# Half of tile 0's first product from words, the first low words of W on POOL, one form kept through the ring's tiles, and gate's first sums after T1's load

## The chip, the core and the metric

The kernel runs on one core of one Trainium2 chip. The engines of a core run side by side and wait for each other by semaphores: PE multiplies matrices, DVE and ACT compute elementwise and read PSUM, POOL (GpSimd) computes elementwise on SBUF alone and issues some transfers, and SP issues the other transfers (DMA). The metric is the device time of one execution in microseconds (us), as the median of several runs.

## The reference

One block: layer norm, linear attention with 32 heads, a gated feed-forward part, and a residual.

```python
xn = _layernorm(x, axis=-1)                    # x: 2048 x 576
# linear attention, H = 32 heads of 18
q, k, v = xn @ wqkv, split by heads
pq, pk = phi(q), phi(k)                        # phi(t) = (t + 1 if t > 0 else exp(t)) + 1e-6
kv = einsum("bhsd,bhse->bhde", pk, v); z = pk summed over s
o = (pq @ kv) / (pq . z + 1e-6)
s = o @ wo
# feed-forward, Df = 4608
g = xn @ w_gate; u = xn @ w_up
g = silu((gelu(g) * u) @ w_down)
return x + s * g
```

## The kernel before

Precision comes from words. A float32 operand is cut into a high word (rounded by ACT to the type fp32r) and a low word (what remains, subtracted by DVE or POOL), and a product is a sum of seven passes of word products. `x_mm_plain` instead multiplies float32 as it is, which takes PE two instructions for each product.

The 2048 rows are 16 tiles of 128, in four blocks of 512. The 576 columns are two halves of 288, so x has parts called B11, B21, B12 and B22 (half j of block b), each held as words (`xo`) and plain (`xf`). W for k and v comes as six pieces (c, j), column group c and half j. The text calls them the first (0, 0), second (0, 1), third (1, 0), fourth (1, 1), fifth (2, 0) and last (2, 1). Their loads are interleaved with those of x.

The order on each engine is the order of the code (`pin` and `keep_in_program_order`), so a step that waits holds all that stands behind it on its engine.

The program has these stages:

1. The head, lines 1266 to 1340: tiles 0 to 2 are normalized (`spread` for the statistics, `scales` for the factor, `center`), turned on PE (`turn`) and cut into words (`place`); `save` copies the plain x. `kv_hi` and `kv_lo` cut W's pieces. `x_mm` makes a tile's k and v products, `k_post` and `v_post` finish them (pk, va), `kv_mm` sums them up. Tile 0 is multiplied plainly for piece c = 0, so it can start before any words are there.
2. Tiles 2 to 7 in `kv_tile`. From tile 4 on a tile is turned only in its mean and factor (ms), and normalized on DVE (`normalize`, within `place`).
3. The q phase for blocks 0 and 1: eight `q_store`, each a product on PE and a phi on ACT, DVE and POOL (e_q, ph). The table `behind` says what is recorded after each. There lie the forms: a form is a sum of x's parts (T1, T2, T3, T4 for the fast matrix product later), cut into words by `build` in the big buffer 12 and kept in device memory by `keep`. There too lie the preparations of tiles 8 to 11.
4. Tiles 8 to 15 and the q phase for blocks 2 and 3.
5. The s phase: attention's output `s_mm` for four blocks of four tiles. The table `aside` says what is recorded after each. `den` computes a block's denominators and writes their words (`aux`); `scale` and `halve` use them; `back` loads a kept form; `mat_sums(0)` forms, on POOL, the sums of gate's first matrix.
6. The gate and up matrices, then the down products.

Short-lived tiles come from rings: `slot` gives one of four tiles under the tag h (pk, va, and later pq), `bank` one of six PSUM banks.

Of the kernel before, what the change touches and what calls it, by code (L numbers as in the profile page):

```python
# [8 lines left out]
F32 = mybir.dt.float32  # L9
# [7 lines left out]
P = 128  # L17
# [8 lines left out]
TBN = S // TB  # L26
# [64 lines left out]
def block_kernel(ctx, tc, x, xe, xt, wq_d, wkv_d, wo, wgu_d, wd_d, out):  # L91
# [6 lines left out]
    def bank(name):  # L98
        return ps.tile([P, 512], F32, tag="one", bufs=6, name=name)
# [10 lines left out]
    def slot(shape, dt, name):  # L110
        return sb.tile(shape, dt, tag="h", bufs=4, name=name)
# [15 lines left out]
    def mm(*args, **kw):  # L127
        pin(nc.tensor.matmul(*args, **kw))  # L128
# [24 lines left out]
    def load_x(n, k):  # L153

        if n % 2 == 0:
            shape = [P, 2, 2, 3 * P] if n < TT else [P, 2, D + 6 * P]
            xstat[n // 2] = big(14 + n // 2 % 2, shape, F32, f"x_{n}")
        t = xstat[n // 2][:, n % 2 : n % 2 + k]
        if n < TT:
            dma(out=t, in_=xe[n * P : (n + k) * P].rearrange("(t p) j d -> p t j d", p=P))  # L160
        else:
            dma(out=t[:, :, 0:D], in_=x[n * P : (n + k) * P].rearrange("(t p) d -> p t d", p=P))
            dma(out=t[:, :, D:], in_=xt[n : n + k].rearrange("t p m -> p t m"))
# [32 lines left out]
    def center(n):  # L196

        if n >= TT:
            return
        xs = xstat[n // 2][:, n % 2]  # L200
        m, r = scale_of.pop(n)
        vec("tensor_scalar", xs, xs, m, r, op0=ALU.subtract, op1=ALU.mult)

    def turn(n, new=bank):

        xs = xstat[n // 2][:, n % 2]
        if n >= TT:
            xts[n] = t = bank(f"ms_{n}")
            for i, v in enumerate(scale_of.pop(n)):
                pin(nc.tensor.transpose(  # L210
                    t[:, i * P : (i + 1) * P], v.to_broadcast([P, P]), ident
                ))
            return
        tiles = [new(f"xt_{n}_{j}") for j in range(2)]
        xts[n] = [t[:, 0 : 3 * P].rearrange("p (k t) -> p k t", k=3) for t in tiles]
        for j in range(2):
            for k in range(3):
                pin(nc.tensor.transpose(xts[n][j][:, k, :], xs[:, j, k * P : (k + 1) * P], ident))
# [22 lines left out]
    def place(n, js=(0, 1), words=(0, 1)):  # L241

        tb, t = divmod(n, TT)
        s, b = divmod(tb, 2)
        c = slice(t * P, (t + 1) * P)
        if n >= TT:
            normalize(n, s, b, c)
            return
        for j in js:
            nm = BS[b][j]  # L250
            if nm not in xo[s]:
                xo[s][nm] = big(2 * b + j, [P, 5, TBN], F32R, f"xo_{s}_{nm}")
            o, v = xo[s][nm], xts[n][j]
            if 0 in words:
                act(o[:, 0:3, c], v, AF.Copy)
            if 1 in words:
                vec("tensor_sub", o[:, 3:5, c], v[:, 0:2, :], o[:, 0:2, c].bitcast(F32))
                r = slice(KR, 2 * KR)
                vec("tensor_sub", o[r, 2, c], v[r, 2, :], o[r, 2, c].bitcast(F32))

    def save(n, js=(0, 1), last=True):

        tb, t = divmod(n, TT)
        s, b = divmod(tb, 2)
# [57 lines left out]
    def load_kv(c, j):  # L322
        n = KV.index((c, j))
        if n % 2 == 0:
            raws["kv", n // 2] = big((2, 3, 12)[n // 2], [P, 2, 3, TM], F32, f"rw_{n}")
        raws[c, j] = raws["kv", n // 2][:, n % 2, :, 0 : TW[c]]
        dma(out=raws[c, j], in_=wkv_d[c, j][:, :, 0 : TW[c]])

    def kv_hi(c, j):
        n = KV.index((c, j))  # L330
        if n < 5:
            act(wkv[n][:, 0:3, 0 : TW[c]], raws[c, j], AF.Copy)
        else:
            for i in range(3):
                act(kv_part(c, j, i), raws[c, j][:, i, :], AF.Copy)

    def kv_lo(c, j, eng, mixed=(False, True)):

        n, raw, r = KV.index((c, j)), raws[c, j], slice(2 * KR, 3 * KR)
        if False in mixed:  # L340
            if n < 5:
                hi, lo = (wkv[n][:, i : i + 2, 0 : TW[c]] for i in (0, 3))
                eng("tensor_sub", lo, raw[:, 0:2, :], hi.bitcast(F32))
            else:
                for i in range(2):
                    eng(
                        "tensor_sub", kv_part(c, j, 3 + i), raw[:, i, :],
                        kv_part(c, j, i).bitcast(F32),
                    )
        if True in mixed:  # L350
            o = kv_part(c, j, 2)[r]
            eng("tensor_sub", o, raw[r, 2, :], o.bitcast(F32))
# [48 lines left out]
    KV_PASSES = [(0, 0), (1, 1), (3, 0), (4, 1), (0, 3), (1, 4), (2, 2)]  # L401
    pkv, pks, vas, es, qt = {}, {}, {}, {}, {}

    def x_mm(t, c):

        tb, i = divmod(t, TT)
        s, b = divmod(tb, 2)
        pkv[t, c] = o = bank(f"kv_{t}_{c}")
        for j in range(2):
            for n, (wi, xi) in enumerate(KV_PASSES):  # L410
                mm(
                    o[:, 0 : TW[c]], xo[s][BS[b][j]][:, xi, i * P : (i + 1) * P], kv_part(c, j, wi),
                    start=(j == 0 and n == 0), stop=(j == 1 and n == len(KV_PASSES) - 1),
                )

    def x_mm_plain(js, ks):

        if (0, 0) not in pkv:
            pkv[0, 0] = bank("kv_0_0")
        for j in js:  # L420
            for k in ks:
                r = slice(0, P if k < 2 else KR)
                mm(
                    pkv[0, 0][:, 0 : TW[0]], xf[0][BS[0][j]][r, k, 0:P], raws[0, j][r, k, :],
                    start=(j == 0 and k == 0), stop=(j == 1 and k == 2),
                )

    def k_post(t, c, by_act=False):

        if c == 0:  # L430
            pks[t] = slot([P, D], F32, f"pk_{t}")
            es[t] = tmp([P, D], f"e_k{t}")
        o, e, src = pks[t], es[t], pkv[t, c]
        cs = slice(0, TW[0]) if c == 0 else slice(TW[0], D)
        src = src[:, 0 : cs.stop - cs.start]
        if by_act:
            act(e[:, cs], src, AF.Relu, scale=-1.0)
        else:
            vec("tensor_scalar", e[:, cs], src, 0.0, None, op0=ALU.min)
        vec("tensor_scalar", o[:, cs], src, 0.0, EPS, op0=ALU.max, op1=ALU.add)  # L440
        if c == 1:
            es.pop(t)
            act(e, e, AF.Exp, scale=-1.0 if by_act else 1.0)
            pool("tensor_add", o, o, e)
# [835 lines left out]
    load_kv(2, 0)  # L1280
    load_x(3, 1)
    load_kv(2, 1)

    spread(0, 1)
    kv_hi(0, 0)
    scales(0)
    center(0)
    turn(0, own_bank)
    save(0, (0,), False)
    spread(1, 1)  # L1290
    save(0, (1,), False)
    kv_lo(0, 0, vec)
    x_mm_plain((0,), range(3))
    scales(1)
    center(1)
    x_mm_plain((1,), (0,))
    turn(1)
    x_mm_plain((1,), (1, 2))
    kv_hi(0, 1)
    kv_lo(0, 1, vec)  # L1300
    place(1)
    kv_hi(1, 0)
    kv_lo(1, 0, pool)
    x_mm(1, 0)
    place(0)
    xts.pop(0)
    load_x(4, 2)
    kv_hi(1, 1)
    kv_lo(1, 1, vec)
    save(1)  # L1310
    x_mm(1, 1)
    k_post(0, 0, True)
    k_post(1, 0, True)
    kv_hi(2, 0)
    kv_lo(2, 0, pool)
    kv_hi(2, 1)
    spread(2, 1)
    kv_lo(2, 1, vec)
    scales(2)
# [13 lines left out]
    v_post(0, 2)  # L1333
    center(3)
    v_post(1, 2)
    make_masks()

    def x_next(n):

# [45 lines left out]
    def form(nm):  # L1385
        keep(0, nm, build(0, nm, 12))

    behind = {
        (0, 0): [lambda: kv_mm(N0 - 1), lambda: spread(N0, 2), lambda: difference(0, 3)],
        (0, 1): [  # L1390
            lambda: scales(N0), lambda: form("T1"), lambda: q_store(1, 4),
        ],
        (0, 3): [lambda: turn(N0)],
        (1, 0): [lambda: form("T3"), lambda: place(N0)],
        (1, 1): [lambda: spread(N0 + 2, 2), lambda: scales(N0 + 2)],
        (1, 2): [lambda: form("T2")],
    }
    for tb in range(2):
        for gi in range(NHG - 1):
# [38 lines left out]
    def first_matrix():  # L1438
# [12 lines left out]
        (3, 1): [lambda: scale(0, 0, 1), lambda: halve(0, 0, 1), lambda: back("B11")],  # L1451
        (3, 2): [lambda: scale(0, 2, 3, 4), lambda: halve(0, 2, 3, 4)],
        (3, 3): [lambda: build(1, "T4", X_SLOT["T4"]), lambda: back("T2")],
        (0, 0): [lambda: den(1), lambda: mat_sums(0)],
        (0, 1): [lambda: scale(1, 0, 1), lambda: halve(1, 0, 1)],
        (0, 2): [lambda: scale(1, 2, 3, 4), lambda: halve(1, 2, 3, 4)],
        (0, 3): [lambda: back("T1")],
        (1, 0): [lambda: pieces.extend(first_matrix()), lambda: run(pieces[0])],
        (1, 1): [lambda: run(pieces[3])],
    }  # L1460
# [79 lines left out]
```

## Time and profile before

| | us |
|---|---|
| median of 3 runs | 1469.98 |
| lowest and highest | 1468.36, 1470.25 |
| profiled execution, its own time | 1467.89 |
| its span in the trace | 1466.2 |
| POOL busy | 578.2 |
| first DMA landing read by DVE | 3.98 |

A row of the timeline has the start in us, the length in us, the engine, the line (often a helper's: 122 is ACT's, 125 DVE's, 128 PE's, 131 POOL's, 134 the DMA's), the operation, output<-input by the program's names, shapes, and how many such instructions follow each other. Brackets say how long the engine stood idle before, and what ended it; "issue" means that the profile shows nothing it waited for. A wait is listed as engine, line, what it waited for, us in total, times and longest. A row of the stages has the stretch, its length, the busy time and count of each engine, the granted clock of PE, the DMA engines' busy share and GB/s. PEld is PE's weight load.

### The profile page before, as it was taken

How to read it: one execution, taken by the hardware profiler on the slowest of the kernel's cores; microseconds unless marked ns; L12 is line 12 of the kernel's file. 1: busy time of each engine (PE TensorE's matmuls, PEld its weight loads, DVE VectorE, ACT ScalarE, POOL GpSimd, SP SyncE). 2: the span in 40 equal slices, each digit the busy share in tenths (PEclk: the TensorE clock that was granted, in tenths of full speed). 3: DMA queues.
4: the chain of work that ended last, by engine and by line, in shares of the span. 5: the costliest groups of instructions: out<-in, count | busy, mean ns of one | idle time of the engine just before them, and what ended most of it. 6: DMA issues, size and time to landing. Idle time of an engine off the chain costs nothing.

```text
span 1466.2 us, 21844 instructions
## 1 busy us (share of the span) xinstructions
PE 1454.2 (99%) x8130; PEld 1296.8 (88%) x8130; DVE 1152.6 (79%) x1602; ACT 561.1 (38%) x911; POOL 578.2 (39%) x513
## 2 busy tenths in 40 slices
PE   9999999999999999999999999999999999999998
PEld 7988989988888888888888888888889999999998
DVE  7678577466878788878778887778788988989897
ACT  5344255432232332322333223322335556545454
POOL 3342340125755666656675665757632000000000
PEclk9999999999999999999999999999999999999999
DMA  5445005442243324334152242323379888867886
GB/s 200 181 177 207 11 2 186 166 166 87 94 151 108 111 84 138 110 114 135 51 180 94 94 141 78 148 87 107 137 257 350 267 258 252 252 186 234 278 289 217
DMA packets 117636, 233.96 MB, mean 160 GB/s; under 512 B 10954, under 2 KB 44362, under 8 KB 115482
## 3 DMA queue, kind: packets, MB, share of 16 engines
q1 hardware_dynamic: 114874, 220.51, 45.0%
q0 software_dynamic: 2656, 12.06, 2.2%
q8 instruction: 64, 1.05, 0.3%
q14 instruction: 42, 0.34, 0.1%
HBM read 149.91 MB, written 82.58 MB: 159 GB/s over the span
## 4 chain that ended last, share of the span: by engine, by line
PE 95%; DVE 3%; ACT 1%; issue 1%; POOL 0%; ACTq 0%; DVEq 0%; POOLq 0%
PE bd L128 24%; PE al L807 16%; PE ga L807 16%; PE de L807 16%; PE be L807 8%; PE kv L128 7%; PE s L128 4%; PE q L128 3%; PE kv_a L128 1%; DVE sx L125 1%; PE d L128 0%; PE kw L128 0%; PE idle L1272 0%; PE b L128 0%; ACT xo_T L122 0%
## 5 line engine op out<-in xcount | busy, mean ns | idle before, releaser
L131 POOL TENSOR_TENSOR sm<-raw 128x384 f32<-128x384 f32 x72 | 75.5, 1048 | 148.6 <-DMA raw<-in_wgu_dram 112.2
L128 PE MATMUL kv<-wkv,xo_B 128*128 128x388 f32 (+2 forms) x658 | 127.5, 349 | 2.7 <-ACT xo_B L122 2.6
L125 DVE TENSOR_TENSOR wa<-sm,wa 128x768 fp32r<-128x768 f32 x72 | 95.1, 1321 | 36.1 <-ACT wa L122 35.3
L128 PEld LDWEIGHTS kv<-wkv,xo_B 128*128 128x128 f32 x658 | 118.8, 188 | 4.6 <-ACT xo_B L122 3.0
L128 PE MATMUL bd<-w_head,hi 128*128 128x288 f32 x516 | 117.9, 294 | 0.0
L125 DVE TENSOR_TENSOR wa<-raw,wa 128x256 fp32r<-128x256 f32 x72 | 68.1, 945 | 50.7 <-ACT wa L122 49.6
L125 DVE TENSOR_TENSOR wb<-raw,wb 128x256 fp32r<-128x256 f32 (+1 forms) x108 | 101.0, 935 | 7.4 <-ACT wb L122 5.8
L122 ACT ACTIVATE hi<-raw_h 128x1024 fp32r<-128x1024 f32 x59 | 62.4, 1059 | 92.8 <-PE bd L128 66.3
L128 PE MATMUL bd<-w_end,hi 128*128 128x288 f32 x448 | 89.8, 294 | 0.0
L122 ACT ACTIVATE spot_h<-spot_h 128x512 f32<-128x512 f32 x49 | 30.8, 633 | 149.4 <-DVE spot_h L125 149.4
L125 DVE TENSOR_TENSOR raw_h<-raw_h,hi 128x1024 fp32r<-128x1024 f32 x59 | 71.8, 1220 | 19.5 <-ACT hi L122 19.4
L128 PEld LDWEIGHTS bd<-w_head,hi 128*128 128x128 f32 x516 | 87.0, 188 | 0.1
L128 PE MATMUL bd<-w_end,raw_h 128*128 128x288 f32 x264 | 77.9, 295 | 0.0
L122 ACT ACTIVATE wa<-sm 128x1152 fp32r<-128x1152 f32 x36 | 41.8, 1161 | 91.0 <-PE de L807 91.0
L122 ACT ACTIVATE u<-al 128x512 f32<-128x512 f32 x72 | 41.0, 592 | 90.0 <-PE al L807 65.1
L128 PEld LDWEIGHTS bd<-w_end,hi 128*128 128x128 f32 x448 | 71.9, 188 | 0.0
L128 PE MATMUL bd<-beside,raw_h 128*128 128x288 f32 x240 | 70.8, 295 | 0.0
L131 POOL TENSOR_TENSOR spot_h<-spot_h,spot_h 128x512 f32<-128x512 f32 x45 | 62.6, 1397 | 2.9 <-DVE spot_h L125 2.4
L807 PE MATMUL al<-xo_B,wa 128*128 128x512 f32 x252 | 63.0, 389 | 0.0
L807 PE MATMUL de<-xo_T,wa 128*128 128x512 f32 x252 | 63.0, 389 | 0.0
L807 PE MATMUL ga<-xo_B,wb 128*128 128x512 f32 x252 | 63.0, 389 | 0.0
L807 PE MATMUL de<-xo_T,wb 128*128 128x512 f32 x252 | 63.0, 389 | 0.0
(270 smaller groups left out, 4058.5 us busy)
## 6 DMA issues: line engine op xcount, KB each, us to landing
raw_h<-hs SPq DMA_DIRECT2D x176, 256.0 KB
raw<-in_wgu_dram SPq DMA_DIRECT2D x36, 768.0 KB
hs<-spot_h SPq DMA_DIRECT2D x90, 256.0 KB
hs<-spot_g SPq DMA_DIRECT2D x80, 256.0 KB
b<-in_wd_dram SPq DMA_DIRECT2D x42, 432.0 KB
hs<-spot_m SPq DMA_DIRECT2D x38, 256.0 KB
raw_g<-hs SPq DMA_DIRECT2D x22, 256.0 KB
kept_T<-xo_T SPq DMA_DIRECT2D x4, 1280.0 KB
```

Source lines behind the costliest of these rows:

```text
L122: pin(nc.scalar.activation(*args, **kw))
L125: pin(getattr(nc.vector, op)(*args, **kw))
L128: pin(nc.tensor.matmul(*args, **kw))
L131: pin(getattr(nc.gpsimd, op)(*args, **kw))
L807: nc.tensor.matmul(o, w[0:rows, wi, :], xop[0:rows, xi, :], start=(start and n == 0), stop=(n == len(PASSES) - 1), skip_group_check=True,)
```

## The change

In the head, half 0 of tile 0 is still multiplied plainly, as the first three products; half 1 comes from words, after tile 1 has been turned, by `x_mm` with `js=(1,)` and the passes in an order that asks for W's low words late. The first low words of W, (0, 0), are cut by POOL in place of DVE, and the masks are made at POOL's start. Half 1 of tile 0 is placed before tile 1, half 0 after W's fourth piece, and the copies `save` come after W's last piece.

```diff
+    make_masks()
     spread(0, 1)
     kv_hi(0, 0)
     scales(0)
     center(0)
+    kv_lo(0, 0, pool)
     turn(0, own_bank)
     save(0, (0,), False)
     spread(1, 1)
-    save(0, (1,), False)
-    kv_lo(0, 0, vec)
-    x_mm_plain((0,), range(3))
+    place(0, (1,), (0,))
     scales(1)
     center(1)
-    x_mm_plain((1,), (0,))
+    place(0, (1,), (1,))
+    x_mm_plain()
+    kv_hi(0, 1)
     turn(1)
-    x_mm_plain((1,), (1, 2))
-    kv_hi(0, 1)
     kv_lo(0, 1, vec)
-    place(1)
     kv_hi(1, 0)
     kv_lo(1, 0, pool)
+    place(1)
+    x_mm(0, 0, (1,), sorted(KV_PASSES, key=lambda i: (i[0] > 1) + (i[0] == 2)))
     x_mm(1, 0)
-    place(0)
-    xts.pop(0)
-    load_x(4, 2)
     kv_hi(1, 1)
     kv_lo(1, 1, vec)
-    save(1)
+    place(0, (0,))
+    load_x(4, 2)
     x_mm(1, 1)
+    kv_hi(2, 0)
+    kv_lo(2, 0, pool)
     k_post(0, 0, True)
     k_post(1, 0, True)
-    kv_hi(2, 0)
-    kv_lo(2, 0, pool)
     kv_hi(2, 1)
+    save(0, (1,))
+    save(1)
...
-    make_masks()
```

In the q phase T3 moves up by three q products and is made in three tiles of the ring h in place of buffer 12, with three transfers out. T2 moves up to the place before the statistics of tile 10.

```diff
+    def form_apart(nm):
+
+        f = xf[0][nm]
+        store[0, nm] = d = dr.tile([P, 5, TBN], F32, name=f"kept_0_{nm}")
+        hi, lo, last = (slot([P, 2, TBN], F32R, f"xo_0_{nm}_{i}") for i in range(3))
+        act(hi, f[:, 0:2], AF.Copy)
+        act(last[:, 0], f[:, 2], AF.Copy)
+        vec("tensor_sub", lo, f[:, 0:2], hi.bitcast(F32))
+        r = slice(KR, 2 * KR)
+        vec("tensor_sub", last[r, 0], f[r, 2], last[r, 0].bitcast(F32))
+        dma(out=d[:, 0:2], in_=hi.bitcast(F32))
+        dma(out=d[:, 3:5], in_=lo.bitcast(F32))
+        dma(out=d[:, 2], in_=last[:, 0].bitcast(F32))
...
     behind = {
         (0, 0): [lambda: kv_mm(N0 - 1), lambda: spread(N0, 2), lambda: difference(0, 3)],
...
+        (0, 2): [lambda: form_apart("T3")],
         (0, 3): [lambda: turn(N0)],
-        (1, 0): [lambda: form("T3"), lambda: place(N0)],
-        (1, 1): [lambda: spread(N0 + 2, 2), lambda: scales(N0 + 2)],
-        (1, 2): [lambda: form("T2")],
+        (1, 0): [lambda: place(N0)],
+        (1, 1): [lambda: form("T2"), lambda: spread(N0 + 2, 2), lambda: scales(N0 + 2)],
     }
```

In the s phase gate's first sums move from the first tile of block 0 to its last, behind the load of T1 on POOL.

```diff
-        (0, 0): [lambda: den(1), lambda: mat_sums(0)],
+        (0, 0): [lambda: den(1)],
...
-        (0, 3): [lambda: back("T1")],
+        (0, 3): [lambda: back("T1"), lambda: mat_sums(0)],
```

The order of the instructions shows the moves. In the head, DVE before, from tile 1's statistics on (wkv_71 is the first piece's words, wkv_72 the second's, x_119 the plain x of tiles 0 and 1, xt_0 and xt_1 their turned halves):

```order
L125 TENSOR_SCALAR st_163<-mv_159 128x1
L125 TENSOR_TENSOR wkv_71<-rw_121,wkv_71 128x832
L125 TENSOR_TENSOR wkv_71<-rw_121,wkv_71 32x416
L125 TENSOR_SCALAR st_163<-st_163 128x1 x3
L125 TENSOR_SCALAR x_119<-x_119,mv_159,st_163 128x768
L125 TENSOR_TENSOR wkv_72<-rw_121,wkv_72 128x832
L125 TENSOR_TENSOR wkv_72<-rw_121,wkv_72 32x416
L125 TENSOR_TENSOR xo_B_193<-xt_0_180,xo_B_193 128x2x128
```

and now:

```order
L125 TENSOR_SCALAR st_173<-mv_169 128x1
L125 TENSOR_SCALAR st_173<-st_173 128x1 x3
L125 TENSOR_SCALAR x_119<-x_119,mv_169,st_173 128x768
L125 TENSOR_TENSOR xo_B_177<-xt_1_159,xo_B_177 128x2x128
L125 TENSOR_TENSOR xo_B_177<-xt_1_159,xo_B_177 32x128
L125 TENSOR_TENSOR wkv_72<-rw_121,wkv_72 128x832
L125 TENSOR_TENSOR wkv_72<-rw_121,wkv_72 32x416
L125 TENSOR_TENSOR xo_B_203<-xt_0_190,xo_B_203 128x2x128
```

The first piece's two low-word instructions are gone from DVE, and the low words of tile 0's half 1 stand ahead of the second piece's. POOL at the same place now (wkv_73 is the third piece's words):

```order
L559 MEMSET small 64x160
L131 TENSOR_TENSOR wkv_71<-rw_121,wkv_71 128x832
L131 TENSOR_TENSOR wkv_71<-rw_121,wkv_71 32x416
L131 TENSOR_TENSOR wkv_73<-rw_125,wkv_73 128x2x412
L131 TENSOR_TENSOR wkv_73<-rw_125,wkv_73 32x412
L131 TENSOR_TENSOR wkv_75<-rw_130,wkv_75 128x2x388
L131 TENSOR_TENSOR wkv_75<-rw_130,wkv_75 32x388
```

POOL begins with the masks, then cuts the first, the third and the fifth piece in a row; before, it had only the latter two, with the masks between them. In the q phase, DVE before, from the statistics of tile 10 to tile 9's normalizing (ph are the phi results, xo_T_1153 is T2, x_664 the plain x of tiles 8 and 9):

```order
L125 SCALAR_TENSOR_TENSOR st_1124<-st_1124 128x2
L125 TENSOR_SCALAR ph_2_1131<-q_2_1132 128x512
L125 TENSOR_TENSOR xo_T_1153<-xf_B_530,xo_T_1153 128x1024
L125 TENSOR_TENSOR xo_T_1153<-xf_B_530,xo_T_1153 32x512
L125 TENSOR_SCALAR ph_3_1159<-q_3_1160 128x512
L125 TENSOR_SCALAR e_k_1200<-kv_0_1181 128x416
L125 TENSOR_SCALAR pk_1199<-kv_0_1181 128x416
L125 TENSOR_TENSOR x_664<-x_664,ms_1196 128x768
```

and now:

```order
L125 SCALAR_TENSOR_TENSOR st_1139<-st_1139 128x2
L125 TENSOR_SCALAR ph_2_1146<-q_2_1147 128x512
L125 TENSOR_SCALAR ph_3_1168<-q_3_1169 128x512
L125 TENSOR_SCALAR e_k_1209<-kv_0_1190 128x416
L125 TENSOR_SCALAR pk_1208<-kv_0_1190 128x416
L125 TENSOR_TENSOR x_668<-x_668,ms_1205 128x768
```

T2's two instructions no longer stand between the last two ph; they stand ahead of tile 10's statistics.

More of the change, by code (lines that the diff above doesn't have):

```diff
@@ L402, in block_kernel, with x_mm, x_mm_plain @@
     pkv, pks, vas, es, qt = {}, {}, {}, {}, {}
-    def x_mm(t, c):
+    def x_mm(t, c, js=(0, 1), passes=KV_PASSES):
         tb, i = divmod(t, TT)
         s, b = divmod(tb, 2)
-        pkv[t, c] = o = bank(f"kv_{t}_{c}")
-        for j in range(2):
-            for n, (wi, xi) in enumerate(KV_PASSES):
+        if 0 in js:
+            pkv[t, c] = bank(f"kv_{t}_{c}")
+        o = pkv[t, c]
+        for j in js:
+            for n, (wi, xi) in enumerate(passes):
                 mm(
                     o[:, 0 : TW[c]], xo[s][BS[b][j]][:, xi, i * P : (i + 1) * P], kv_part(c, j, wi),
-                    start=(j == 0 and n == 0), stop=(j == 1 and n == len(KV_PASSES) - 1),
+                    start=(j == 0 and n == 0), stop=(j == 1 and n == len(passes) - 1),
                 )
[L416 to L426, printed above, removed]
+    def x_mm_plain():
+        pkv[0, 0] = bank("kv_0_0")
+        for k in range(3):
+            r = slice(0, P if k < 2 else KR)
+            mm(
+                pkv[0, 0][:, 0 : TW[0]], xf[0][BS[0][0]][r, k, 0:P], raws[0, 0][r, k, :],
+                start=(k == 0), stop=False,
+            )
     def k_post(t, c, by_act=False):
```

## The prediction

> **What bounds the kernel now.** I read the page first, then the waits of PE, then the timeline around each wait.
>
> ```profile
> span 1466.2 us, 21844 instructions
> PE 1454.2 (99%) x8130; PEld 1296.8 (88%) x8130; DVE 1152.6 (79%) x1602; ACT 561.1 (38%) x911; POOL 578.2 (39%) x513
> ```
>
> PE is busy 1454.2 of 1466.2 us, so a change can gain only where PE works less or waits less. The list of PE's waits says where it waits after its start:
>
> ```profile
> PE kv L128 <- ACT xo_B L122: 2.6, 1, 2.6
> ...
> PE xt L218 <- issue: 0.6, 1, 0.6
> PE b L128 <- DVE aux L125: 0.4, 1, 0.4
> ```
>
> There are three waits of any size, 3.6 us together, and the change touches all three places. From the gate phase to the end PE's order is the same, so I take that as unchanged.
>
> **First part: the head (0 to 26 us).** Who sets its length is read from DVE and PE.
>
> ```profile
> 8.23 1.62 DVE L125 TENSOR_TENSOR wkv<-rw,wkv 128x832 fp32r<-128x832 f32 x2
> 9.89 0.71 DVE L125 TENSOR_SCALAR st<-st 128x1 f32<-128x1 f32 x3
> 10.63 0.68 DVE L125 TENSOR_SCALAR x<-x,mv,st 128x768 f32<-128x768 f32 x1
> 11.23 1.61 DVE L125 TENSOR_TENSOR wkv<-rw,wkv 128x832 fp32r<-128x832 f32 x2
> 12.87 1.51 DVE L125 TENSOR_TENSOR xo_B<-xt,xo_B 128x256 fp32r<-128x256 f32 x4
> ...
> 20.78 3.12 DVE L125 TENSOR_TENSOR wkv<-rw,wkv 128x388 fp32r<-128x388 f32 x3
> ...
> 24.67 0.68 DVE L125 TENSOR_SCALAR x<-x,mv,st 128x768 f32<-128x768 f32 x1
> ```
>
> ```profile
> 8.34 3.45 PE L128 MATMUL kv<-rw,xf_B 128*128 128x416 f32 x8 [0.25 <-ACT xf_B L122]
> ...
> 13.97 10.93 PE L128 MATMUL kv<-wkv,xo_B 128*128 128x416 f32 x56
> 25.45 0.84 PE L218 MATMUL xt<-ident,x 128*128 128x128 f32 x6 [0.56 <-issue]
> ```
>
> DVE runs nearly without a gap to 25.35, when x of tile 2 is centered, and 0.1 us later PE turns it. PE stood 0.56 us before that. So the head ends when DVE's chain ends. Removing PE work alone gains at most that PE waits longer.
>
> PE's saving: the plain product takes 12 instructions, 8.34 to 13.97 less six transposes (0.65), 0.415 each. The change makes six of them (2.5) into seven products of words at 10.73/56 = 0.19 (1.33): 1.17 us less work. DVE's saving: the first 1.62 us above go to POOL. What POOL then does to DVE shows here:
>
> ```profile
> 93.75 1.29 POOL L131 TENSOR_TENSOR ph<-ph,e_q 128x512 f32<-128x512 f32 x1 [3.07 <-DVE st L125]
> 93.90 1.16 DVE L125 SCALAR_TENSOR_TENSOR st<-st 128x2 f32<-128x2 f32 x1
> ```
>
> ```profile
> 14.23 1.98 POOL L131 TENSOR_TENSOR wkv<-rw,wkv 128x824 fp32r<-128x824 f32 x1 [12.53 <-ACT wkv L122]
> 16.07 1.02 DVE L125 TENSOR_TENSOR wkv<-rw,wkv 128x824 fp32r<-128x824 f32 x1
> 16.29 1.74 POOL L131 TENSOR_TENSOR wkv<-rw,wkv 32x412 fp32r<-32x412 f32 x1
> 17.12 1.35 DVE L125 TENSOR_TENSOR wkv<-rw,wkv 32x412 fp32r<-32x412 f32 x1
> 21.66 1.23 POOL L131 TENSOR_TENSOR wkv<-rw,wkv 32x388 fp32r<-32x388 f32 x1
> ```
>
> A DVE instruction on two elements with two SBUF inputs took 1.16 us: it ended 0.02 after POOL's addition. In the second fence the two alternate: POOL's 16.29 runs 0.94 past DVE's end at 17.09, DVE's 17.12 runs 0.44 past POOL's end at 18.03. I read: such instructions exclude each other for their whole length, and who has waited goes next. The Trainium skill (SBUF — State Buffer, Who interferes with whom) states this as a rule: DVE and GpSimd share one port pair under an exclusive lock. The trace agrees (1.16 us for two elements). It speaks against this change: by it the two engines cannot halve W's words between them, and the head loses; by shared bandwidth without a lock it would gain (first rival).
>
> When each can start is read from ACT and the loads:
>
> ```profile
> 5.58 1.23 ACT L122 ACTIVATE wkv<-rw 128x1248 fp32r<-128x1248 f32 x1
> ...
> 8.50 0.20 ACT L122 ACTIVATE st<-st 128x1 f32<-128x1 f32 x1
> ...
> 8.98 1.23 ACT L122 ACTIVATE wkv<-rw 128x1248 fp32r<-128x1248 f32 x1
> ...
> 12.91 1.24 ACT L122 ACTIVATE wkv<-rw 128x1236 fp32r<-128x1236 f32 x1
> ```
>
> ```profile
> 0.00:9.20 9.20, 6.44 (x37) 5.68 (x38) 4.50 (x13) 4.29 (x9) 0.96 (x8) 1.00 0.80 292
> ```
>
> The first five loads are 2.70 MB by their shapes; 292 GB/s over 9.2 us moved 2.69. So the third of W is there near 10, and ACT, which no longer stands behind turn(1), rounds it right after the second: 10.1 to 11.34.
>
> The new chain. POOL takes the first low words at 6.9 (or 7.1), 2.0 and about 1.0 us, to 10.1. DVE has tile 1's factor at 9.48 (ACT's 8.70 plus three steps), and its centering, which reads and writes SBUF whole, I let wait for POOL as the 128x824 rows do: 10.65; without that wait, 10.15. PE is not held: its three plain products end at 10.83. Low words of tile 0's half: to 11.33. Then W's second low words start, 1.02 to 12.35, and POOL, with the third of W since 11.42, goes between the two instructions until 14.25. DVE's second one ends at 14.7. The mixed product of tile 0 waits for it: **PE, ready at 12.6, stands until 14.7** and starts tile 1 at 14.9 instead of 13.97.
>
> From 14.7 on DVE: tile 1's low words (1.5) 16.2; W's fourth behind POOL's 128x776 (an estimate of 1.86 from the 1.98, so to 17.5), 0.9, POOL's 0.9, 0.44, to 19.7; tile 0's other half 0.75; pk and statistics as before 2.3, to 22.8; W's last three meet no POOL now, 1.7 instead of 3.12, to 24.5; factor and centering 1.4, to 25.95. PE is there at 25.6. So turn(2) moves from 25.45 to about 26.0: **+0.5**. The masks, moved to POOL's start, lie in the 12.53 us in which it idled there, and the copies of x, moved back on ACT, have no reader before the q phase: nothing. Bounds: -1.1 (no exclusion: 1.62 less, and 0.5 of it lost to ACT's 8.70) and +1.6 (POOL first at 11.4, second rival). I take +0.5 because both starts that decide it come from rows.
>
> **Second part: the q phase.**
>
> ```profile
> 105.17 1.92 DVE L125 TENSOR_TENSOR xo_T<-xf_B,xo_T 128x1024 fp32r<-128x1024 f32 x2 [1.36 <-ACT xo_T L122]
> ```
>
> ```profile
> 114.53 5.31 PE L128 MATMUL kv<-wkv,xo_B 128*128 128x412 f32 x28
> 115.14 1.48 ACT L122 ACTIVATE xo_T<-xf_B 128x1536 fp32r<-128x1536 f32 x1
> 116.65 1.92 DVE L125 TENSOR_TENSOR xo_T<-xf_B,xo_T 128x1024 fp32r<-128x1024 f32 x2 [1.35 <-ACT xo_T L122]
> 118.60 0.69 DVE L125 TENSOR_SCALAR ph<-q 128x512 f32<-128x512 f32 x1
> ...
> 120.31 0.95 DVE L125 TENSOR_TENSOR x<-x,ms 128x768 f32<-128x768 f32 x1
> ...
> 122.47 0.83 PE L128 MATMUL kv<-wkv,xo_B 128*128 128x416 f32 x3 [2.63 <-ACT xo_B L122]
> ```
>
> PE ends tile 8 at 119.84 and waits 2.63 us for tile 9's words. Tile 9 is normalized only at 120.31, since T2's form stood in front of the last ph. With T2 gone from there, ACT takes the last e_q at 115.14 instead of xo_T, about 0.6 long, and ph follows at 115.75, not 118.60: 2.85 earlier. Normalizing starts at 117.46 and PE, 2.16 after it as now, could start at 119.62, before it is ready: **-2.6**, with 0.2 to spare.
>
> That holds if the ph ahead of it does not slip. T3's form leaves the place in front of tile 8 (1.92 and 1.36 of waiting, 3.28); T2's enters in front of tile 10's statistics with the same 1.48 on ACT and 1.92 on DVE, and may wait for one POOL addition (1.29, partly over by then). I call that even. T3's new place is covered: DVE waits 1.50 us there now and more behind it. It issues three transfers on SP where one stood, some 10 us earlier, ahead of ph's stores and two x loads, which nobody needs for 20 us or more. The ring's tiles that it takes are wanted again by tile 8's pk and va, after 115, some 14 us behind its transfers. If the cover is short, each us late comes back on PE. Bounds: -2.63 and, two additions met, -0.3.
>
> **Third part: gate's first sums.**
>
> ```profile
> 245.23 1.28 DVE L125 TENSOR_TENSOR aux<-r,aux 32x128 fp32r<-32x128 f32 x4 [0.44 <-ACT aux L122]
> ...
> 262.69 2.52 DVE L125 TENSOR_TENSOR aux<-r,aux 32x128 fp32r<-32x128 f32 x4 [0.43 <-ACT aux L122]
> ...
> 265.27 0.72 PE L128 MATMUL b<-aux 128*128 128x512 f32 x2 [0.45 <-DVE aux L125]
> ```
>
> ```profile
> 274.32 0.58 POOL L134 DMA_DIRECT2D xr_T<-kept_T  x1 [9.89 <-PE s L128]
> ```
>
> ```profile
> 282.14 1.17 ACT L122 ACTIVATE wa<-sm 128x1152 fp32r<-128x1152 f32 x1
> ```
>
> The four small subtractions of den(1), the lower row, took 1.24 us more than those of den(0), since POOL formed the sums beside them; 0.45 of it reached PE. The sums now stand behind the load of T1 (274.9) and take 4 x 1.0, to 279; ACT reads them first at 282.14. **-0.45**; nothing of it can be lost unless that load slips by 3 us.
>
> **Sum.** 0.5 - 2.6 - 0.45 = -2.55 against the profiled execution's own 1467.89, its span of 1466.2 and 1.7 around it: 1465.3. The median of the runs shown, 1469.98, lies 2.09 above that execution, so I forecast 1467.4.
>
> **Rivals.**
> 1. *The head gains.* POOL and DVE overlap; DVE's chain loses 1.62 and 0.5 of it is idle: -1.1 in place of +0.5, 1465.8. For it: DVE bounds the head and loses work. Against: every two-input pair in the rows above excluded each other. 0.18.
> 2. *POOL comes first at 11.4.* The two starts are 0.1 us apart. Then POOL runs to 13.4, DVE 0.9, POOL 0.9, DVE 0.44 to 15.7 and the head costs +1.6: 1468.5. 0.18.
> 3. *Tile 9's wait only shrinks.* The change does not do what it says in the q phase: T2's form before tile 10's statistics makes ACT's Ln, the next e_q and ph late, behind POOL's additions. Two of these (2.6) less 0.2 to spare leave 0.3 of the gain: 1469.7. 0.12.
> 4. *The exclusion costs more than all gains: slower.* The same mechanism in full, in both phases: POOL's six word instructions of the head (9 us) each hold DVE from tile 1's centering on, 6.9 us of waits instead of the 2.6 now, with 1.1 gained elsewhere: +3.1; and three additions met in the q phase (3.9) turn -2.6 into +1.1. With -0.45 that is +3.7: 1473.7. It is slower from the point where DVE waits for POOL some 2.6 us longer than I count. Against: DVE also has instructions from PSUM that pass POOL. 0.10.
>
> **How the numbers follow.** The forecast has 0.42. A measurement of this kernel can tell about 0.2% from no change, so faster means below 1467.04 and slower above 1472.92. The forecast lies just inside, and the three runs spread over 1.9 us: 0.17 of it faster, 0.25 same. Rival 1 gives 0.17 faster, 0.01 same; rival 2 0.03 and 0.15; rival 3 0.02 and 0.10; rival 4 0.01 same and 0.09 slower. Faster 0.39, same 0.52, slower 0.09. The range goes from rival 1 less 0.9 of spread, 1464.9, to rival 3 plus 0.7, 1470.4; the forecast's own is 1466.2 to 1468.6.
>
> **What would show it.** Right: a wait of PE near 12.6 to 14.7 on DVE's wkv, a POOL wkv between the two DVE instructions of W's second low words, turn(2) near 26.0; no wait of PE near 120 and tile 9's x near 117.5; aux at 1.28 in den(1). Wrong: turn(2) before 25.0 (rival 1) or after 26.6 (rival 2 or 4), a PE wait at 119.8 above 0.5 us (rival 3). A new wait in the gate phase would refute the claim that the rest is unchanged.

## The result and the profile after

| | before | after |
|---|---|---|
| median, us | 1468.43 of 7 runs | 1464.52 of 7 runs |
| lowest to highest, us | 1468.06 to 1470.25 | 1464.15 to 1465.24 |
| profiled execution, own time, us | 1467.89 | 1464.87 |
| its span, us | 1466.2 | 1463.2 |

The change makes the kernel faster by 3.9 us; the ratio of the runs is 0.9970 with a 95% interval of 0.9959 to 0.9982. The forecast was 1467.4 with a range from 1464.9: the time lies just below the range. The profiled execution itself was forecast at 1465.3 and measured 1464.87.

The page after, first the span and the engines' busy time:

```profile
span 1463.2 us, 21853 instructions
PE 1453.6 (99%) x8131; PEld 1298.0 (89%) x8131; DVE 1151.9 (79%) x1600; ACT 561.2 (38%) x912; POOL 582.3 (40%) x515
```

PE is busy 0.6 us less than before (1454.2); the other 2.4 of the 3.0 us came out of its waits. The list of its waits after:

```profile
PE kv L128 <- DVE wkv L125: 1.6, 1, 1.6
PE idle L1272 <- POOL ident masks.py:199: 1.6, 1, 1.6
PE xt L218 <- DVE x L125: 0.6, 1, 0.6
PE kv L128 <- ACT xf_B L122: 0.3, 1, 0.3
PE xt L218 <- PE idle L1272: 0.2, 1, 0.2
```

The waits of 2.6 us (tile 9) and 0.4 us (the denominators' words) are gone. New is 1.6 us on DVE's words of W in the head. The timeline of the head after, for PE, DVE and POOL:

```profile
14.58 10.97 PE L128 MATMUL kv<-wkv,xo_B 128*128 128x416 f32 x57 [1.60 <-DVE wkv L125]
26.20 0.87 PE L218 MATMUL xt<-ident,x 128*128 128x128 f32 x6 [0.65 <-DVE x L125]
```

```profile
11.26 3.27 DVE L125 TENSOR_TENSOR wkv<-rw,wkv 128x832 fp32r<-128x832 f32 x2
...
16.10 3.88 DVE L125 TENSOR_TENSOR wkv<-rw,wkv 128x824 fp32r<-128x824 f32 x2
...
23.06 1.62 DVE L125 TENSOR_TENSOR wkv<-rw,wkv 128x388 fp32r<-128x388 f32 x3
```

```profile
11.89 3.57 POOL L131 TENSOR_TENSOR wkv<-rw,wkv 128x824 fp32r<-128x824 f32 x2 [1.73 <-ACT wkv L122]
```

DVE's pair on W's second piece took 3.27 us in place of 1.61 before, the pair on the fourth 3.88 in place of 2.40 (1.02 and 1.35 with a small gap): POOL's instructions go between them. The three on the last piece took 1.62 in place of 3.12, for they meet no POOL now. The first turn of tile 2 moved from 25.45 to 26.20.

The q phase after:

```profile
109.78 2.46 DVE L125 TENSOR_TENSOR xo_T<-xf_B,xo_T 128x1024 fp32r<-128x1024 f32 x2 [0.77 <-ACT xo_T L122]
...
118.10 0.94 DVE L125 TENSOR_TENSOR x<-x,ms 128x768 f32<-128x768 f32 x1
```

```profile
115.33 7.94 PE L128 MATMUL kv<-wkv,xo_B 128*128 128x412 f32 x42
```

Tile 9 is normalized at 118.10 in place of 120.31, and PE runs through its end of tile 8 (28 products in the row of before) and tile 9's first 14 in one row, without a wait. The s phase after:

```profile
260.63 1.28 DVE L125 TENSOR_TENSOR aux<-r,aux 32x128 fp32r<-32x128 f32 x4 [0.43 <-ACT aux L122]
```

```profile
275.14 1.02 POOL L131 TENSOR_TENSOR sm<-raw,sm 128x384 f32<-128x384 f32 x1
```

```profile
279.37 1.17 ACT L122 ACTIVATE wa<-sm 128x1152 fp32r<-128x1152 f32 x1
```

The four small subtractions are back at 1.28 us, and the sums end at 276.2, 3.2 us before ACT reads them.

The three terms, +0.75, -2.63 and -0.45, make -2.33. The span fell by 3.0 in the two profiled executions, and the median by 3.9. The experiments ask for the difference, and for the part that each edit has in it.

### The profile page after: what moved, and what is told of

It is laid out like the page before. It is cut to its first block, busy times and chain, and to the rows that moved or that the text cites. A ratio compares the mean times of both kernels' runs of the same rounds, so it can differ in the third digit from the quotient of the medians.

```text
span 1463.2 us, 21853 instructions
## 1 busy us (share of the span) xinstructions
PE 1453.6 (99%) x8131; PEld 1298.0 (89%) x8131; DVE 1151.9 (79%) x1600; ACT 561.2 (38%) x912; POOL 582.3 (40%) x515
## 4 chain that ended last, share of the span: by engine, by line
PE 95%; DVE 3%; DMA 1%; issue 1%; ACT 1%; SPq 0%; DVEq 0%; ACTq 0%
PE bd L128 24%; PE al L807 16%; PE ga L807 16%; PE de L807 16%; PE be L807 8%; PE kv L128 7%; PE s L128 4%; PE q L128 4%; PE kv_a L128 1%; DVE sx L125 1%; DVE wkv L125 0%; DMA x<-in_xe_dram 0%; DVE xo_B L125 0%; DVE acc L125 0%; PE d L128 0%
## 5 line engine op out<-in xcount | busy, mean ns | idle before, releaser
L128 PE MATMUL kv<-wkv,xo_B 128*128 128x416 f32 (+2 forms) x665 | 129.1, 349 | 1.6 <-DVE wkv L125 1.6
L807 PE MATMUL al<-xr_B,wa 128*128 128x512 f32 x252 | 63.0, 389 | 0.0
```

Source lines behind the costliest of these rows:

```text
L807: nc.tensor.matmul(o, w[0:rows, wi, :], xop[0:rows, xi, :], start=(start and n == 0), stop=(n == len(PASSES) - 1), skip_group_check=True,)
```

## The experiments

E1 to E4 ran on one chip, E5 to E8 on a second and E9 to E12 on a third, each beside runs of the kernel before on that chip; a median is compared with that of its own chip. The median of before was 1469.93 (24 runs, 1467.82 to 1471.49) beside E1 to E4, 1470.11 (16 runs, 1467.89 to 1471.58) beside E5 to E8, and 1469.73 (26 runs, 1467.79 to 1471.31) beside E9 to E12.

### E1: the head alone

The edit is the head's part of the diff, on the kernel before:

```diff
     center(0)
+    kv_lo(0, 0, pool)
     turn(0, own_bank)
...
+    place(1)
+    x_mm(0, 0, (1,), sorted(KV_PASSES, key=lambda i: (i[0] > 1) + (i[0] == 2)))
     x_mm(1, 0)
```

> Only the head is changed, the q phase and the sums are as before. Theory A (the terms add up as the trace of the change shows them: head +0.75, q phase -2.6, sums -0.45): the first turn of tile 2 moves from 25.45 to about 26.2 us and the time rises by 0.5 to 1.0 us. Rival B (the later start at tile 2 is absorbed before tile 9, because tile 9's wait is set by DVE and not by PE): the wait before tile 9 shrinks from 2.63 to about 1.9 us and the time stays within 0.3 us. On the median: theory P (the three runs before lay high by chance) expects the kernel before at 1468.0 to 1468.8 in these rounds; rival Q (the kernel before really alternates between about 1468.3 and 1470, two runs in three at the upper one) expects its median at or above 1469.5.

Measured: 1470.62, 0.7 us above before; the ratio is 1.0007 (0.9998 to 1.0016). Its turn of tile 2:

```profile
25.90 0.87 PE L218 MATMUL xt<-ident,x 128*128 128x128 f32 x6 [0.56 <-DVE x L125]
```

This is 0.45 later than before, where theory A expected 0.75 (26.2), and PE's wait before tile 9 is still 2.63, so the head's loss is not absorbed there: theory A holds in direction, rival B falls. The size is not settled by the interval, which reaches to no loss. The median of before is no chance of three runs, so theory P falls; rival Q's bound holds, but its runs spread over 3.7 us and do not jump between two values.

This profile shows more. Its stages of 1 us around the wait (the number ahead of the last two is PE's granted clock), and PE's first product of tile 9:

```profile
121.00:122.00 1.00, 0.00 (x0) 0.00 (x0) 0.96 (x2) 0.00 (x0) 0.19 (x1) 1.00 1.14 481
122.00:123.00 1.00, 0.03 (x1) 0.03 (x1) 0.88 (x3) 0.61 (x2) 0.00 (x0) 0.76 0.81 338
123.00:124.00 1.00, 1.00 (x3) 0.97 (x4) 0.94 (x3) 0.38 (x1) 0.00 (x0) 0.50 0.85 271
124.00:125.00 1.00, 1.00 (x5) 0.95 (x4) 0.94 (x4) 0.09 (x1) 0.00 (x0) 0.50 0.70 141
125.00:126.00 1.00, 1.00 (x5) 0.95 (x4) 0.05 (x1) 1.00 (x3) 0.33 (x1) 0.53 1.00 377
126.00:127.00 1.00, 1.00 (x7) 0.99 (x6) 0.00 (x0) 0.42 (x3) 1.00 (x1) 1.00 1.00 379
```

```profile
122.97 4.26 PE L128 MATMUL kv<-wkv,xo_B 128*128 128x416 f32 x14 [2.63 <-ACT xo_B L122]
```

The same in the profiled execution of before, on which the forecast was built:

```profile
123.00:124.00 1.00, 1.00 (x7) 0.99 (x6) 0.91 (x4) 0.00 (x0) 0.00 (x0) 1.00 0.85 133
124.00:125.00 1.00, 1.00 (x7) 0.99 (x6) 0.54 (x2) 0.60 (x2) 0.00 (x0) 1.00 0.86 237
```

```profile
122.47 2.90 PE L128 MATMUL kv<-wkv,xo_B 128*128 128x416 f32 x14 [2.63 <-ACT xo_B L122]
```

After the same wait of 2.63 us the granted clock fell to 0.50 for some 3 us in one execution and stayed at 1.00 in the other. The 14 instructions took 4.26 us in place of 2.90, so this wait cost 1.36 us more than its length. The reader is to see that the page of before cannot show it: its one execution was one without the fall.

### E2: the q phase alone

```diff
+        (0, 2): [lambda: form_apart("T3")],
         (0, 3): [lambda: turn(N0)],
-        (1, 0): [lambda: form("T3"), lambda: place(N0)],
-        (1, 1): [lambda: spread(N0 + 2, 2), lambda: scales(N0 + 2)],
-        (1, 2): [lambda: form("T2")],
+        (1, 0): [lambda: place(N0)],
+        (1, 1): [lambda: form("T2"), lambda: spread(N0 + 2, 2), lambda: scales(N0 + 2)],
```

> Only the q phase is changed (T3 apart in the ring's tiles, T2 in front of tile 10's statistics). Theory A: the wait of 2.63 us before tile 9 is gone, the time falls by 2.5 to 2.9 us. Rival B (without the head's later start DVE is late for tile 9 again, since PE arrives 0.75 us earlier): some 0.5 us of that wait is left and the time falls by about 2.1 us.

Measured: 1465.54, 4.4 us below before; the ratio is 0.9972 (0.9961 to 0.9982). The wait before tile 9 is gone whole, so rival B falls, but 4.4 is more than both theories allow. What is over 2.63, some 1.8, is near E1's 1.36. Its runs lie within 2.0 us (1464.03 to 1466.0), those of before within 3.7.

### E3: gate's first sums alone

```diff
-        (0, 0): [lambda: den(1), lambda: mat_sums(0)],
+        (0, 0): [lambda: den(1)],
...
-        (0, 3): [lambda: back("T1")],
+        (0, 3): [lambda: back("T1"), lambda: mat_sums(0)],
```

> Only gate's first sums are moved. Theory A: the wait of 0.45 us on the denominators' words is gone and nothing else moves: -0.3 to -0.6 us, at the edge of what can be told from no change. Rival: the extra 0.7 us by which the whole change fell more than the three terms together comes from this part (the sums no longer hold DVE elsewhere in the s phase): -1.0 to -1.3 us.

Measured: 1469.63, 0.3 us below before; the ratio is 0.9997 (0.9988 to 1.0005), no difference that can be told. In its profile the wait on the denominators' words is gone, as theory A says; the median does not bear out -1.0 or more, though the interval reaches that far. It too has the wait of 2.64 before tile 9, with the clock behind it at half, and the 14 products take 4.48 us in place of 2.90:

```profile
124.00:125.00 1.00, 1.00 (x5) 0.96 (x4) 0.88 (x4) 0.19 (x1) 0.00 (x0) 0.50 0.65 83
125.00:126.00 1.00, 1.00 (x5) 0.96 (x4) 0.00 (x0) 1.00 (x4) 0.43 (x1) 0.50 1.03 353
```

```profile
122.87 4.48 PE L128 MATMUL kv<-wkv,xo_B 128*128 128x416 f32 x14 [2.64 <-ACT xo_B L122]
```

### E4 and E8: the change without its head

The q phase's and the sums' edits, with the head of before; twice, the second time beside the whole change.

> The change without its head. Theory A: 0.6 to 0.9 us below the whole change, that is -4.3 to -4.8 us against the kernel before if the whole change is -3.9. Rival B (the head's part is worth nothing or a gain): the same as the whole change or slower, -3.9 us or less.

> The change without its head once more, now beside the whole change on one chip. Theory A (the head costs 0.5 to 0.75): 0.4 to 0.9 us below the whole change. Rival B (the head costs nothing): within 0.3 us of it.

Measured: 1464.98 (ratio 0.9971, 0.9960 to 0.9983) and 1464.71 (0.9963, 0.9951 to 0.9976), that is 4.95 and 5.4 us below before. Beside the whole change (E7, 1465.10) it is 0.4 us lower, the lower end of what theory A allows, with intervals that overlap. The turn of tile 2 starts at 25.54 in E8's profile and at 26.20 after. But this is no clean comparison either: in E4, which has the same head as E8, it starts at 26.18, and in E5 below, which also has the head of before, at 26.16, since there tile 1's x reached DVE 0.9 us late:

```profile
7.92 0.82 DVE L125 BATCH_NORM_STATS2 bn<-x 128x6 f32<-128x288 f32 x2 [0.93 <-DMA x<-in_xe_dram]
```

```profile
26.16 0.85 PE L218 MATMUL xt<-ident,x 128*128 128x128 f32 x6 [0.54 <-issue]
```

So the arrival of a load moves the same head by as much as the change does. E1, where DVE waits for no load of tile 1's x, as before, is the fairest pair: 0.45 lost. The two medians (0.7 in E1, 0.4 here) point the same way; that the head is a loss is likely, and not shown clear of the noise.

### E5 and E12: work in PE's wait

E1 made a new theory, here called C: the spread of the kernel before is the clock's fall behind the 2.63 us, and the change gains it besides. To test it, the wait's end is left as it is, and PE is given work that nobody reads, in the bank that the next product overwrites:

```diff
         pkv[t, c] = o = bank(f"kv_{t}_{c}")
+        if (t, c) == (9, 0):
+            for _ in range(20):
+                pin(nc.tensor.transpose(o[:, 0:P], ident, ident))
```

E12 has 8 in place of 20.

> The kernel before with one addition: 20 transposes of the identity (about 0.11 us each, some 2.2 us of work that nobody reads) stand on PE in front of tile 9's first product, in the 2.63 us in which PE waits there; they go to the bank that this product overwrites. Theory C (PE's idle 2.63 us let its granted clock fall to half for some 3 us in many executions, which costs up to 1.8 us in each of these; the change gains this too, and the profiled execution of before was one without it): the fastest runs stay at 1467.8 to 1468.4, the slow ones near 1470 to 1471.5 go, and the median falls by 1.0 to 1.9 us though PE waits for the same instruction as before. Rival D (the spread of the kernel before has another cause, such as the start or the loads): median and spread as before, within 0.5 us.

> The kernel before with 8 transposes in place of 20 in front of tile 9's first product, so that about 1.7 us of PE's wait is left in one piece. Theory C in its strict form (any idle stretch of this size lowers the clock): runs up to 1470.5 and a median of 1469.5 or more, as in the kernel before. Theory C with a threshold between 1.7 and 2.6 us, which the waits of 1.6 us in the head of the whole change speak for (its clock showed 1.00 there): median 1468.3 to 1469.2 and no run above 1470, as with 20 transposes.

Measured: 1468.98 with 20, 1.1 us below before (runs 1468.21 to 1469.52; ratio 0.9992, 0.9983 to 1.0001), and 1468.47 with 8, 1.3 us below (1467.90 to 1469.50; ratio 0.9993, 0.9984 to 1.0002). The intervals just reach 1, but the spread decides: of the runs of before, 10 of 16 and 14 of 26 lie above 1469.6, of these 22 none. The mean granted clock, on record for each run to 0.001, says the same: of the 66 runs of before on the three chips the 19 with 0.998 all took 1469.9 or more and the 17 with 1.000 at most 1469.53; E1, E3 and E9, which keep the wait, have runs at 0.998 and 0.997 too, and of the 73 runs of the kernels in which the wait is gone or filled none is below 0.999. PE around tile 9 with 20 and with 8:

```profile
120.38 2.35 PE L411 MATMUL kv<-ident 128*128 128x128 f32 x20
123.18 2.91 PE L128 MATMUL kv<-wkv,xo_B 128*128 128x416 f32 x14 [0.45 <-ACT xo_B L122]
```

```profile
119.81 1.03 PE L411 MATMUL kv<-ident 128*128 128x128 f32 x8
122.59 2.91 PE L128 MATMUL kv<-wkv,xo_B 128*128 128x416 f32 x14 [1.75 <-ACT xo_B L122]
```

PE starts tile 9 when ACT lets it, as before, and useless work made the kernel's median lower. So theory C holds, rival D falls; and the strict form of C falls as well: 1.75 us in one piece left no run in the upper group. The length from which the clock can fall lies between 1.75 and 2.63 us.

### E7: the whole change again

> The whole change once more, on the chip of its neighbours. Theory A with C (the profiled terms -2.3 and the half clock of before, which its median holds and the change does not): 3.3 to 5.5 us below the kernel before by the medians, and a spread of its own runs below 2 us where before has over 3. Without C: 2.3 to 3.0 us below.

Measured: 1465.10, 5.0 us below before; the ratio is 0.9969 (0.9957 to 0.9981). This is within 3.3 to 5.5, as A with C says. The spread is 2.7 us, not below 2: four runs lie at 1464.19 to 1465.43 and two at 1466.74 and 1466.88. The profile is of one of the latter. Its head, on ACT, POOL, DVE and PE:

```profile
6.77 1.25 ACT L122 ACTIVATE wkv<-rw 128x1248 fp32r<-128x1248 f32 x1 [1.11 <-DMA rw<-in_wkv_dram]
```

```profile
12.18 3.76 POOL L131 TENSOR_TENSOR wkv<-rw,wkv 128x824 fp32r<-128x824 f32 x2 [0.93 <-ACT wkv L122]
```

```profile
10.10 1.57 DVE L125 TENSOR_SCALAR x<-x,mv,st 128x768 f32<-128x768 f32 x1
...
12.35 4.04 DVE L125 TENSOR_TENSOR wkv<-rw,wkv 128x832 fp32r<-128x832 f32 x2
```

```profile
16.44 10.82 PE L128 MATMUL kv<-wkv,xo_B 128*128 128x416 f32 x57 [0.72 <-DVE wkv L125]
```

W's first load came 1.1 us later, so POOL's first low words did, DVE's centering waited for them (1.57 us in place of 0.68), and POOL got W's third piece 0.17 us before DVE could start the second. That is the prediction's second rival. It cost PE a second wait, and the turn of tile 2 starts at 27.10 there, 0.9 us later than in the profile after. The change's head thus has a second outcome, and in this one profile a load's arrival decided it; part of the 0.9 is the start itself, since the first turn was at 7.67 there and at 7.12 after.

### E6 and E11: POOL's shorter instruction first

On the whole change, the order of POOL's two instructions on W's third piece is turned round; in E11 also on the fifth:

```diff
-    kv_lo(1, 0, pool)
+    kv_lo(1, 0, pool, (True,))
+    kv_lo(1, 0, pool, (False,))
```

> The whole change with POOL's two instructions on the third piece of W in the other order, the 32x412 first and the 128x824 behind it. By the exclusion of DVE and POOL, DVE's second instruction on the second piece waits 0.9 instead of 1.8 us and ends near 13.65 instead of 14.52, PE's wait of 1.60 falls to 0.6 to 0.9, DVE does the fourth piece between POOL's third and fifth, and tile 2's turn moves from 26.20 to between 25.1 and 25.6: 0.6 to 1.1 us less than the whole change. Rival (POOL and DVE share bandwidth without a lock, so the order within POOL's work does not matter): PE's wait of 1.60 and the time stay within 0.2 us.

> The whole change with POOL's two instructions in the other order for the third piece of W and for the fifth. Theory A: DVE's second instruction on the fourth piece waits 0.9 us for POOL in place of 1.8 and tile 2's turn comes up to 0.3 us earlier than with the third piece's alone (PE's last wait there was 0.31 us): 1463.2 or 0 to 0.4 us below that kernel, and 1.2 to 2.0 us below the whole change. Rival: no further gain, since PE's own work sets the head by then.

Measured: 1463.48 (ratio to before 0.9957, 0.9945 to 0.9970), 1.6 us below the whole change on the same chip, and 1463.19 in E11 (0.9956, 0.9944 to 0.9969). DVE and PE in E6's head:

```profile
11.31 2.41 DVE L125 TENSOR_TENSOR wkv<-rw,wkv 128x832 fp32r<-128x832 f32 x2
```

```profile
13.77 10.75 PE L128 MATMUL kv<-wkv,xo_B 128*128 128x416 f32 x57 [0.49 <-DVE wkv L125]
24.82 0.87 PE L218 MATMUL xt<-ident,x 128*128 128x128 f32 x6 [0.31 <-DVE x L125]
```

DVE's pair ends at 13.72 (13.65 was expected) in place of 14.53, PE's wait is 0.49 in place of 1.60, and the turn starts at 24.82, 1.38 before the whole change's, more than the 1.1 expected. POOL does the same work in the same two instructions; only their order changed, so the lock explains it and shared bandwidth does not. In E11 the turn starts at 24.27 with no wait ahead of it. Beside E6's that is 0.55 us in the trace, but the spans are both 1461.5, since E11 has a wait of 0.6 us in the gate phase that E6 has not, and the medians come from two chips: that the second turn gains is not shown. E11 is the lowest median of all, 6.5 us below before; E6 is 6.6 below its own.

### E9 and E10: the two forms apart

In E9 T2 alone moves, in E10 T3 alone:

```diff
-        (1, 1): [lambda: spread(N0 + 2, 2), lambda: scales(N0 + 2)],
-        (1, 2): [lambda: form("T2")],
+        (1, 1): [lambda: form("T2"), lambda: spread(N0 + 2, 2), lambda: scales(N0 + 2)],
```

```diff
+        (0, 2): [lambda: form_apart("T3")],
...
-        (1, 0): [lambda: form("T3"), lambda: place(N0)],
+        (1, 0): [lambda: place(N0)],
```

> Of the q phase only T2's move: T2 stands in front of tile 10's statistics, T3 stays in front of tile 8 in buffer 12. Theory A (both forms share buffer 12, so T2 can be made there only once T3's transfer to device memory has read it, and the move needs T3 out of the buffer): ACT stands several us on that transfer in front of tile 10's statistics, the last e_q and ph come late, tile 9's wait on PE stays at 1 to 4 us, and the time is within 1.5 us of the kernel before. Rival (T2's place alone makes the gain): the wait before tile 9 is gone and the time falls by 3.5 to 5 us like that of the whole q phase.

> Of the q phase only T3's move into the ring's tiles; T2 stays in front of the last ph. Theory A with C: DVE still stands 3 us in T2's form in front of tile 9's normalizing, PE's wait before tile 9 stays at 2.0 to 2.7 us, so the half clock stays too, with runs spread over 3 us, and the median is within 0.6 us of the kernel before. Rival (T3's leaving the place in front of tile 8 is what gains): -2 to -4.5 us.

Measured: E9 1472.55, 2.8 us slower than before (ratio 1.0021, 1.0013 to 1.0030). ACT waits for T3's transfer out of buffer 12, and PE for ACT:

```profile
113.36 1.49 ACT L122 ACTIVATE xo_T<-xf_B 128x1536 fp32r<-128x1536 f32 x1 [2.44 <-DMA kept_T<-xo_T]
```

```profile
124.80 4.78 PE L128 MATMUL kv<-wkv,xo_B 128*128 128x416 f32 x14 [4.88 <-ACT xo_B L122]
```

The mechanism is theory A's, though the wait is longer than its 4 us and the loss larger than its 1.5. The 14 products behind it took 4.78 us in place of 2.90, the clock's fall again (0.50 from 122.1 to 128.9). E10 is the surprise: 1465.65, 4.1 us faster (ratio 0.9973, 0.9964 to 0.9982), with T2 where it was. DVE there:

```profile
113.37 1.92 DVE L125 TENSOR_TENSOR xo_T<-xf_B,xo_T 128x1024 fp32r<-128x1024 f32 x2 [1.35 <-ACT xo_T L122]
...
117.04 0.95 DVE L125 TENSOR_TENSOR x<-x,ms 128x768 f32<-128x768 f32 x1
```

T2's form still stands ahead of the last ph and still costs DVE 1.92 and 1.35, but all of it begins 3.3 us earlier, since T3's form no longer stands ahead of tile 8. Tile 9 is normalized at 117.04 in place of 120.31, which is 3.27. Theory A falls here and its rival holds: T3's move alone makes the q phase's gain.

## Why the prediction was wrong, and where it was right

**The step that failed** is the last one of the sum: "The median of the runs shown, 1469.98, lies 2.09 above that execution, so I forecast 1467.4". The 2.09 was taken for something that the change leaves alone, as a time around the span would be. After the change the median lies 0.35 below its profiled execution, so 2.44 of the 2.88 us by which the forecast missed come from this term; the sum itself missed by 0.4 (1465.3 for the profiled execution, which took 1464.87). The range's low end, rival 1's time less the spread, had the 2.09 in it as well.

E1, E3, E5 and E12 show where much of such an offset comes from: behind PE's wait of 2.63 us the granted clock falls to half in many executions (24 of the 42 runs of before beside E5 and E12 lie above every run with the wait filled), and the change removes that wait. So in the executions with the fall the change gains the wait and the fall, and in the profiled one, which had none, the wait alone. That the upper two of the three runs shown (1469.98 and 1470.25) had the fall is inferred from their times, since their clock isn't on record.

The fall is not all of it. Filling the wait lowered the median by 1.1 us (E5) and 1.3 (E12); with the three terms' 2.33 that makes 3.4 to 3.6 of the 5.0 us in E7, and 1.4 to 1.6 stay open. The profiled execution of before was fast in its start too: its turn of tile 2, 25.45, is with E10's the earliest of the nine profiles with that head, the latest being 26.18. And three runs were few: of the seven runs of before in the first comparison three lie above 1469.2, fewer than on the later chips, their median is only 0.54 above the profiled execution, and so the change gained 3.9 us there.

The Trainium skill (TensorE: Matmul & The Clock Gate, Part 1: The HAM clock gate) says that the gate halves PE's clock after an idle window of about 3.4 us, and that the window runs freely. The half clock, its depending on the execution, and the 3.4 us as the time for which the half clock lasts (last section) agree with E1 and E3; that PE must stand idle for that long does not, since 2.63 us were enough here.

**The head** was right in its mechanism, and its size is not known better than the forecast had it. PE's wait for the second low words ended at 14.58 where 14.7 was forecast; DVE's later steps ran up to 0.3 us late (the last piece's words began at 23.06 where 22.8 was said), and the turn came at 26.20 in place of 26.0. In E1's profile the load of W's fifth piece came 0.3 us earlier and the turn did too, at 25.90: +0.45, beside +0.75 after and +0.5 forecast. E6 shows that the lock on DVE and POOL is the cause of PE's wait. The Trainium skill's rule on the lock (SBUF — State Buffer, Who interferes with whom), on which the prediction weighed this, stands: DVE's pair took 3.27 us with POOL's long instruction ahead of its second step and 2.41 with the short one. The bound of +1.6 is real too, as E7's profile shows, and belongs to executions in which a load is late.

**The q phase** was right in its sum, -2.6 against -2.63, and wrong in which edit makes it. The prediction gave the gain to T2's leaving (2.85 us) and called T3's leaving and T2's entering even. The sum allows the other pairing as well, T2's leaving against its entering, with T3's leaving as the gain, and E10 shows that one: T3's leaving gives 3.27 by itself. That the number came out is no proof of the first pairing, since PE could gain no more than its wait of 2.63 either way. After the whole change tile 9 is normalized at 118.10 with a head that is 0.75 later, so 117.35 against E10's 117.04: T2's move gains nothing more, and by E9 it loses without T3's, since both forms are made in buffer 12. The new place of T3 was covered, as forecast.

**The sums** were right: the wait of 0.45 is gone, and they are ready 3.2 us ahead of their reader. E3 cannot tell it from no change in the runs.

**From the gate phase to the end** the prediction took PE as unchanged. In the profile of the change that holds. Yet in E7's a wait stands there that neither of the two first profiles has, shorter ones (0.2 to 0.6 us) in E1's, E4's, E8's, E10's and E11's:

```profile
948.00 1.89 PE L807 MATMUL ga<-xo_B,wb 128*128 128x512 f32 x7 [1.05 <-DVE u L125]
```

Why it comes in some executions was not tried. With the 0.9 us of the head it is about the 1.8 us by which this execution's span (1465.0) is above that of the profile after, and so about the 2 us by which the upper two runs of E7 lie above the rest; the other of the two has no profile. Of the 0.7 us by which the span fell more than the three terms, 0.34 lies between tile 2 and the s phase: PE's product with aux, 265.27 before, starts here at

```profile
262.60 0.63 PE L128 MATMUL b<-aux 128*128 128x512 f32 x2
```

which is 2.67 earlier against -2.33. The rest lies behind it. Starts of whole executions differ as much: the first turn was between 7.09 (E5) and 7.80 (E2). No cause is claimed for it.

**The rivals.** The first (the head gains by overlap) fell: with the change's head the turn of tile 2 came at 25.90, 26.20 and 27.10, and this rival needed it before 25.0. The second occurred in E7's profile. The third (tile 9's wait only shrinks) and the fourth (slower) did not come. By the prediction's own line for faster, below 1467.04, the change is faster, to which it gave 0.39 and to no change 0.52.

## What to carry to other kernels

Look at PE's granted clock behind each of its waits, and at when the first loads land, in more than one execution: a wait of 2.6 us cost up to 1.6 us beyond its length, and filling it in part with work that nobody reads took 1.1 to 1.3 us off the median. When a median stands apart from the profiled execution, ask whether the change removes what sets them apart before adding the difference to a forecast. Where two engines lock each other out, and one of them has its next step waiting, give the other's short instruction the turn ahead of its long one; and where a step is moved, add up everything that stands between its old place and the wait, since leaving one place may be worth more than the place that the edit seems to be about.

## What was not expected of the hardware

PE's clock fell to 0.50 behind an idle stretch of 2.63 us, in some executions of one kernel and not in others, and was not seen to fall behind 1.75 us (E12) or behind the 1.6 us in the head after. Stages of 0.2 us show when. In E1 it fell 2.2 us after PE had stopped, in E9 also 2.2, and in E3 3.0, when PE had been at work again for 0.4 us. It stayed at half for 3.4 us in E1 and E3, and for twice as long, 6.8, behind E9's longer wait. E3's stages in which it falls and comes back:

```profile
123.20:123.40 0.20, 0.20 (x2) 0.20 (x1) 0.17 (x2) 0.08 (x1) 0.00 (x0) 0.60 1.02 399
126.60:126.80 0.20, 0.20 (x2) 0.20 (x1) 0.00 (x0) 0.00 (x0) 0.20 (x1) 0.86 1.10 445
```

These starts and lengths fit a clock that is set anew every 3.4 us by how busy PE was, so that the same wait counts or not by where it lies; no run here tried that.

A DVE instruction with one input, the centering of 128x768, waits for POOL as those with two do, which the prediction assumed without a row for it: 1.57 us in E7, ending 0.42 us after POOL's low words at 11.25, against 0.68 alone.
